# A two-layer expert kernel: the early conditional cast of first-layer weights goes into one arm of the first layer

## The chip, the cores and the metric

The kernel runs on one core of one Trainium2 chip. The metric is the device time of one execution in microseconds (us), the median of several runs.

## The reference

Three layers follow each other: a gated linear attention, a first feed-forward layer (a maximum of three products, then an output product), and a mixture of experts in which each token goes to the one expert whose gate is largest. The change lies in the last.

```python
B, H, S, D = 4, 8, 768, 48                      # attention
state = alpha_t[..., None] * state + k_t (outer) v_t ;  y_t = q_t @ state
x = y.transpose(0, 2, 1, 3).reshape(3072, 384)
x = np.maximum(np.maximum(x @ w1, x @ w2), x @ w3) @ w_out      # 384 -> 768 -> 384

logits = x @ w_gate                              # experts: 8, d_ff = 1024
e_idx = np.argmax(logits, axis=1)
gate_w = probs[np.arange(N), e_idx]              # softmax
eom = 1.0 / (1.0 + np.exp(-(x @ w_output_gate)))
for e in range(8):
    mask = e_idx == e
    h = np.maximum(x[mask] @ w1[e], 0.0)         # 384 -> 1024
    out[mask] = gate_w[mask, None] * eom[mask, e, None] * (h @ w2[e])
```

## The kernel before

The first 484 us compute attention and the first feed-forward layer. The rest is a loop over *slots* `j`: a slot is up to 128 tokens of one expert, in the order of the experts. There are at most `NS` = 31 slots; with these inputs 30 are used, and how many tokens each expert has is known only on the chip.

Products are made in one of two ways. In a slot of more than 64 tokens (*whole*), weights and activations are split into a high and a low part in the fast 32-bit format, and three products stand for one: high by high, high by low, low by high. The split weights of the first layer are `w1H` and `w1L`, one pair of buffers for all slots; `split1` makes them from the staging buffer `s1` by 6 pieces, each a copy on ScalarE (ACT, line 605) and a subtraction on VectorE (DVE, line 606). `w2H`, `w2L`, `s2` and `split2` (8 pieces) do the same for the second layer. A slot whose tokens fit in 64 (*alone*) needs no split weights: it multiplies straight from `s1` and `s2` in plain 32-bit, both halves of the width side by side (`halves`, line 814). Staging buffers are two of each kind, `s1a`/`s1b` and `s2a`/`s2b`, used in turn by even and odd slots, and filled by DMAs that SyncE (SP) issues only if the slot's expert is another than the slot's before (line 775).

What a slot is stands in registers: `kind[j]` is 1 for an alone slot, and `new[j]` tells when the weights of a whole slot with a new expert may be cast: 0 not at all, 1 *late* (the slot before is whole and still reads `w1H`), 2 *early* (the slot before is alone and reads none of it). `cast1(j, when)` is `split1(j)` under `tc.If(new[j] == when)`. A conditional has two arms in the program. In the arm that is skipped, ACT and DVE wait until all that they issued before is finished, and then raise the semaphore by as much as the other arm would have; whoever waits for a cast thus waits for that point where there is no cast.

The order on each engine is the order of the code (`manual_schedule`). One pass of the loop, for slot `j`:

1. `split2(j)`, pieces 0 and 1 (under a conditional, line 1152)
2. `up(j + 1, 0)`: first half of the next slot's first layer, 9 products of TensorE (PE, line 825) into a bank `psM`, copied by ACT (line 826) to `hs`. An alone slot has nothing here.
3. `th(j)`: transposes of `hs` (8 on PE, line 865; 4 in an alone slot, line 870), then ReLU and split into `ch` by two instructions each on ACT (line 844) and DVE (line 845); in an alone slot one ReLU on ACT (line 871)
4. `split2(j)`, pieces 2 to 7 (conditional, line 1162)
5. `cast1(j + 2, 2)`, the early cast (conditional; the records show line 1132 for it)
6. `up(j + 1, 1)`: second half, 9 products, or all 12 of an alone slot (line 814)
7. `tx(j + 2)`: 3 transposes of the gathered tokens (line 788), then `cx` high by ACT (line 793) and low by DVE (line 794)
8. DMA of `s1` of slot `j + 3`
9. `cast1(j + 2, 1)`, the late cast (conditional, line 1132 too)
10. `down(j)`: second layer, 24 products (line 884) or 16 (line 814), scaling by ACT (line 898), for an alone slot one addition of halves (lines 902, 903), and a scatter to the output by GpSimd (POOL, line 904)
11. DMA of `s2` of slot `j + 2`

All `up` products of a whole slot read `w1H` and `w1L`, so they wait for the last place in the program before them that may have written these.

Of the kernel before, what the change touches and what calls it, by code (L numbers as in the profile page):

```python
# [33 lines left out]
NS = NT + NE - 1  # L34
# [50 lines left out]
def layers(tc, pool, wk, K, general, *args):  # L85
    with ExitStack() as ctx:
        _layers(ctx, tc, pool, wk, K, general, *args)


def _layers(ctx, tc, pool_, wk, K, general, qk, al, a0, v, vT, w123, wout, gates, ew1, ew2, out):  # L90
# [25 lines left out]
    def bank(p, tag, name):  # L116
        return p.tile([128, 512], F32, tag=tag, name=name)
# [460 lines left out]
    xg, cx, cxF, hs, ch, chg, new, eos, kind = ({} for _ in range(9))  # L578
# [25 lines left out]
    def split(src, hi, lo):  # L604
        nc.scalar.copy(hi, src)
        nc.vector.tensor_sub(lo, src, hi.bitcast(F32))

    def split1(j, pieces=range(6)):
        for n in pieces:
            split(*(t[:, n % 3, n // 3 * 512:(n // 3 + 1) * 512] for t in (C["s1"][j % 2], *C["w1"])))  # L610

    def split2(j, pieces=range(NE)):
        for f in pieces:
            split(*(t[:, f] for t in (C["s2"][j % 2], *C["w2"])))
# [148 lines left out]
    def load_meta(j):  # L763
        chg[j] = nc.values_load(kinds[0:1, 2 * NS + j:2 * NS + j + 1], engines=(ET.SP,), min_val=0, max_val=1)
        eos[j] = nc.values_load(meta[0:1, j:j + 1], engines=(ET.SP,), min_val=0, max_val=NE - 1)

    def load_kind(j):
        kind[j] = nc.values_load(kinds[0:1, j:j + 1], engines=(ET.PE, ET.Activation, ET.DVE),
                                 min_val=0, max_val=1)
        new[j] = nc.values_load(kinds[0:1, NS + j:NS + j + 1], engines=(ET.Activation, ET.DVE),  # L770
                                min_val=0, max_val=2)
# [6 lines left out]
    def gather(j):  # L778
        xg[j] = C["cr"].tile([128, XW], F32, tag="xg", name="xg", bufs=4)
        n = TF * 128 if j < NF else NTOK  # L780
        nc.gpsimd.indirect_dma_start(out=xg[j], out_offset=None, in_=x2d[:n, :],
                                     in_offset=bass.IndirectOffsetOnAxis(ap=gidx[:, j:j + 1], axis=0),
                                     bounds_check=n - 1, oob_is_err=False)

    def tx(j):
        ps = bank(C["psT"], "T", "psT")
        for k in range(3):
            nc.tensor.transpose(ps[:, k * 128:(k + 1) * 128], xg[j][:, k * 128:(k + 1) * 128], ident)
        cx[j] = bp.tile([128, 2, DM], F32R, tag=("xH", "xL")[j % 2], name="cx")
        cxF[j] = bp.tile([128, DM], F32, tag="hH", name="cxF", bufs=7)  # L790

        def parts(hi, lo, p):
            nc.scalar.copy(hi, p)
            nc.vector.tensor_sub(lo, p, hi.bitcast(F32))  # L794

        def alone():
            nc.scalar.copy(cxF[j], ps[:, :DM])

        by_kind(j, lambda: parts(cx[j][:, 0], cx[j][:, 1], ps[:, :DM]), alone)

    def by_kind(j, whole, alone):
        if j not in kind:
            return whole()
        with tc.If(kind[j] == 1) as c:
            alone()
        with c.Else():
            whole()
# [4 lines left out]
    def halves(ps, n, x, w, start, stop):  # L812
        for g in range(2):
            mm(ps[64 * g:64 * g + 64, :n], x[g], w[g], start=start, stop=stop, skip_group_check=True)

    def up(j, h):
        w1H, w1L = C["w1"]
        fs = slice(h * 512, h * 512 + 512)

        def whole():  # L820
            ps = bank(psM, "M", "psM1")
            for k in range(3):
                ks = slice(k * 128, (k + 1) * 128)
                for n, (x, w) in enumerate(((0, w1H), (0, w1L), (1, w1H))):
                    mm(ps, cx[j][:, x, ks], w[:, k, fs], start=(k + n == 0), stop=(k + n == 4))  # L825
            nc.scalar.copy(hs[j][:, fs], ps)  # L826

        def alone():
            ps = bank(psM, "M", "psM1")
            w = C["s1"][j % 2]  # L830
            for k in range(3):
                x = cxF[j][:, k * 128:k * 128 + 64]
                halves(ps, 512, (x, x), [w[:, k, g * 512:(g + 1) * 512] for g in range(2)], k == 0, k == 2)
            nc.scalar.copy(hs[j][:, :512], ps)

        if h == 0:
            hs[j] = bp.tile([128, FF2], F32, tag="x32", name="hs")
            with tc.If(kind[j] == 0) if j in kind else nullcontext():
                whole()
        else:  # L840
            by_kind(j, whole, alone)
# [14 lines left out]
    def th(j):  # L856
        ch[j] = bp.tile([128, 2, FF2], F32R, tag=f"o{j % 2}", name="ch", bufs=1)
        p0 = bank(C["psH"], "H", "psH")

        def whole():  # L860
            p1 = bank(C["psH"], "H", "psH")
            for h, ps in enumerate((p0, p1)):
                for f in range(4):
                    fs = slice((4 * h + f) * 128, (4 * h + f + 1) * 128)
                    nc.tensor.transpose(ps[:, f * 128:(f + 1) * 128], hs[j][:, fs], ident)
                cut(ch[j][:, 0, h * 512:h * 512 + 512], ch[j][:, 1, h * 512:h * 512 + 512], ps)

        def alone():
            for f in range(4):
                nc.tensor.transpose(p0[:, f * 128:(f + 1) * 128], hs[j][:, f * 128:(f + 1) * 128], ident)  # L870
            nc.scalar.activation(hs[j][:, 512:], p0, AF.Relu)

        by_kind(j, whole, alone)

    def down(j, fs=(0, NE)):
        if fs[0] == 0:
            C["dn"] = bank(psM, "M", "psP") if j == 1 else bank(psO, "O", "psP")
        ps = C["dn"]
        w2H, w2L = C["w2"]

        def whole():
            for f in range(*fs):
                for n, (x, w) in enumerate(((0, w2H), (0, w2L), (1, w2H))):
                    mm(ps[:, :DM], ch[j][:, x, f * 128:(f + 1) * 128], w[:, f], start=(f + n == 0),  # L884
                       stop=(f == NE - 1 and n == 2))

        def alone():
            w = C["s2"][j % 2]
            for f in range(4):
                x = hs[j][:, 512 + f * 128:512 + (f + 1) * 128]  # L890
                halves(ps, DM, (x[:, :64], x[:, 64:]), (w[:, f], w[:, f + 4]), f == 0, f == 3)

        by_kind(j, whole, alone)
        if fs[1] < NE:
            return
        y = bp.tile([128, DM], F32, tag="hm", name="yo")
        gate = xg[j][:, DM:XW]
        nc.scalar.activation(y, ps[:, :DM], AF.Copy, scale=gate)  # L898
        if j in kind:
            with tc.If(kind[j] > 0):  # L900
                t = bp.tile([128, DM], F32, tag="hL", name="ylo", bufs=7)
                nc.scalar.copy(t[:64], ps[64:, :DM])
                nc.vector.scalar_tensor_tensor(y[:64], t[:64], gate[:64], y[:64], op0=ALU.mult, op1=ALU.add)
        nc.gpsimd.indirect_dma_start(out=out[:, :], out_offset=bass.IndirectOffsetOnAxis(ap=sidx[:, j:j + 1], axis=0),  # L904
                                     in_=y, in_offset=None, bounds_check=NTOK - 1, oob_is_err=False)
# [222 lines left out]
    def guard(j):  # L1128
        return tc.If(n_all > j) if j >= NT else nullcontext()

    def cast1(j, when):
        with tc.If(new[j] == when):  # L1132
            split1(j)

    down(1, (0, 2))
    tx(2)
    down(1, (2, 5))
# [9 lines left out]
    for j in range(NF, NS):  # L1147
        if j + 3 < NS:
            load_meta(j + 3)
            load_kind(j + 3)  # L1150
        if j > NF:
            with tc.If(new[j] > 0):
                split2(j, range(2))
        if j + 3 < NS:
            gather(j + 3)
        with guard(j):  # L1156
            if j + 1 < NS:
                with guard(j + 1):
                    up(j + 1, 0)
            th(j)  # L1160
        if j > NF:
            with tc.If(new[j] > 0):
                split2(j, range(2, NE))
        if j + 2 < NS:
            cast1(j + 2, 2)
        if j + 1 < NS:
            with guard(j + 1):
                up(j + 1, 1)
                if j + 2 < NS:
                    tx(j + 2)  # L1170
        if j + 3 < NS:
            stage(j + 3, ((0, "s1"),))
        if j + 2 < NS:
            cast1(j + 2, 1)
        with guard(j):  # L1175
            down(j)
        if j + 2 < NS:
            stage(j + 2, ((1, "s2"),))
# [50 lines left out]
```

## Time and profile before

| what | us |
|---|---|
| median of 3 runs (834.53, 840.00, 840.49) | 840.0 |
| the profiled execution | 835.41 |
| its span, from the first to the last instruction | 833.7 |
| PE busy in that span | 746.9 (90%) |
| ACT busy | 307.0 (37%) |
| DVE busy | 380.9 (46%) |

The mean granted clock of PE over the span is 0.957 of full speed; in the slices of the page's second part that fall in the loop it reads 8 or 9 tenths in many, where the stages before it read 9. A matmul's recorded time is longer than the step to the next one, because matmuls overlap; the pace is read from the starts. A row of the timeline names the start, the time, the engine, the line, the operation and its tiles, and in brackets how long the engine stood idle just before and what ended that.

### The profile page before, as it was taken

The page shows a single profiled execution, that of the slowest core. Times are in us where ns is not written, and L with a number is a line of the kernel's source. Part 1 is how long each engine was busy: PE and PEld are TensorE (multiplying, and loading weights), DVE is VectorE, ACT ScalarE, POOL GpSimd, SP SyncE. Part 2 cuts the span into 40 slices and gives each one's busy share as a digit, 9 for nine tenths or more (in the row PEclk, how much of TensorE's full clock was granted, in tenths as well). Part 3 has the DMA queues.
Part 4 walks back from the last instruction along what each step waited for, and adds up shares of the span by engine and source line. Part 5 has one row for each costly group of instructions (what it writes and reads, how often), then busy time and mean ns, then how long its engine had stood idle before and what let it go on. Part 6 is the DMA issues. An engine that isn't in the chain of part 4 may idle for free. (4 is left out here: it accounts for less than half of the span.)

```text
span 833.7 us, 14691 instructions
## 1 busy us (share of the span) xinstructions
PE 746.9 (90%) x4782; PEld 652.7 (78%) x4782; DVE 380.9 (46%) x806; ACT 307.0 (37%) x750; POOL 110.7 (13%) x117
## 2 busy tenths in 40 slices
PE   7889999989999999999999888888879798896882
PEld 7679989878999999999999777777556577763562
DVE  7868784598676474632327621110232311102322
ACT  4364343544434343432314422222444422324342
POOL 1000000010111110100103021011211201111110
PEclk9999999998999999999999999898989989999897
DMA  9732302624104140000004010115936101377450
GB/s 256 293 87 91 131 0 77 183 67 115 54 18 121 37 120 20 17 12 20 8 28 181 23 56 30 30 39 175 335 119 249 32 20 39 114 282 306 145 212 15
DMA packets 23748, 86.63 MB, mean 104 GB/s; under 512 B 7988, under 2 KB 11852, under 8 KB 19536
## 3 DMA queue, kind: packets, MB, share of 16 engines
q1 hardware_dynamic: 18192, 73.24, 26.5%
q0 software_dynamic: 3904, 10.84, 4.1%
q10 hardware_dynamic: 1536, 1.18, 0.6%
q8 instruction: 51, 0.84, 0.4%
q14 instruction: 65, 0.53, 0.2%
HBM read 128.09 MB, written 10.63 MB: 166 GB/s over the span
## 5 line engine op out<-in xcount | busy, mean ns | idle before, releaser
L429 PE MATMUL hps<-xH,wH 128*128 128x384 f32 x432 | 151.4, 350 | 1.8 <-ACT xH L341 1.8
L429 PE MATMUL hps<-xH,wL 128*128 128x384 f32 x432 | 146.1, 338 | 0.7 <-DVE wL L398 0.7
L429 PE MATMUL hps<-xL,wH 128*128 128x384 f32 x432 | 146.2, 339 | 0.4 <-DVE xL L342 0.4
L825 PE MATMUL psM<-w1H,cx 128*128 128x512 f32 x276 | 108.0, 448 | 36.6 <-ACTq L1132 36.6
L884 PE MATMUL psP<-w2H,ch 128*128 128x384 f32 x368 | 103.2, 351 | 1.4 <-ACT ch L844 1.3
L825 PEld LDWEIGHTS psM<-w1H,cx 128*128 128x128 f32 x276 | 57.6, 209 | 56.3 <-ACTq L1132 43.2
L455 POOL TENSOR_TENSOR hL<-hm,hH 128x384 fp32r<-128x384 f32 x36 | 44.8, 1244 | 404.6 <-ACT hH L450 404.5
L429 PEld LDWEIGHTS hps<-xH,wH 128*128 128x128 f32 x432 | 82.1, 190 | 8.4 <-ACT xH L341 2.5
L845 DVE SCALAR_TENSOR_TENSOR ch<-psH,ch 128x512 fp32r<-128x512 f32 x46 | 29.7, 686 | 128.6 <-ACT ch L844 128.2
L429 PEld LDWEIGHTS hps<-xH,wL 128*128 128x128 f32 x432 | 82.2, 190 | 1.0 <-DVE wL L398 1.0
L429 PEld LDWEIGHTS hps<-xL,wH 128*128 128x128 f32 x432 | 82.2, 190 | 0.9 <-DVE xL L342 0.9
L884 PEld LDWEIGHTS psP<-w2H,ch 128*128 128x128 f32 x368 | 69.8, 195 | 2.0 <-ACT ch L844 1.5
L826 ACT COPY hs<-psM 128x512 f32<-128x512 f32 x46 | 26.9, 586 | 117.2 <-PE psM L825 115.3
L825 PE MATMUL psM<-w1L,cx 128*128 128x512 f32 x138 | 62.4, 452 | 7.9 <-DVEq L1132 7.8
L465 PE MATMUL ops<-wo,hH 128*128 128x400 f32 x258 | 68.2, 345 | 0.0
L904 POOL DMA_INDIRECT out<-yo,sidx x30 | 31.2, 1041 | 275.0 <-ACTq L900 161.5
L884 PE MATMUL psP<-w2L,ch 128*128 128x384 f32 x184 | 63.1, 343 | 0.0
L436 DVE TENSOR_TENSOR hm<-hm,hps 128x384 f32<-128x384 f32 x48 | 26.4, 551 | 67.0 <-PE hps L429 63.0
L794 DVE TENSOR_TENSOR cx<-psT,cx 128x384 fp32r<-128x384 f32 x24 | 13.3, 556 | 89.0 <-ACTq L1132 88.9
L450 ACT CAST hH<-hm 128x384 fp32r<-128x384 f32 x43 | 22.0, 512 | 80.9 <-DVE hm L439 77.2
L898 ACT ACTIVATE yo<-psP,xg 128x384 f32<-128x384 f32 x30 | 17.4, 581 | 88.5 <-PE psP L884 65.2
L465 PEld LDWEIGHTS ops<-wo,hH 128*128 128x128 f32 x258 | 46.9, 188 | 0.4
(214 smaller groups left out, 1200.9 us busy)
## 6 DMA issues: line engine op xcount, KB each, us to landing
s1a<-in_ew SPq DMA_DIRECT2D x15, 1536.0 KB
s2a<-in_ew SPq DMA_DIRECT2D x15, 1536.0 KB
s1b<-in_ew SPq DMA_DIRECT2D x14, 1536.0 KB
s2b<-in_ew SPq DMA_DIRECT2D x14, 1536.0 KB
ws<-in_w SPq DMA_DIRECT2D x6, 1152.0 KB
at<-in_al SPq DMA_DIRECT2D x16, 336.9 KB
vt<-in_v SPq DMA_DIRECT2D x8, 576.0 KB
x2d<-xs SPq DMA_DIRECT2D x24, 192.0 KB
```

The costliest lines, as they stand in the source:

```text
L429: mm(ps, slab(a, f)[:, w, k], b[i][:, k], start=(n == 0), stop=(n == 8))
L436: nc.vector.tensor_max(m, m, ps)
L450: nc.scalar.copy(hH[i, f], m)
L455: (nc.gpsimd if general or i > 1 else nc.vector).tensor_sub(hL[i, f], hps["m"], hH[i, f].bitcast(F32))
L465: mm(ps[:, :DM + NG], a[i, f][:, ts_], wo[f // 3][:, b, f % 3], start=(f + n == 0), stop=(f + n == 7))
L794: nc.vector.tensor_sub(lo, p, hi.bitcast(F32))
L825: mm(ps, cx[j][:, x, ks], w[:, k, fs], start=(k + n == 0), stop=(k + n == 4))
L826: nc.scalar.copy(hs[j][:, fs], ps)
L845: nc.vector.scalar_tensor_tensor(lo, ps, 0.0, hi.bitcast(F32), op0=ALU.max, op1=ALU.subtract)
L884: mm(ps[:, :DM], ch[j][:, x, f * 128:(f + 1) * 128], w[:, f], start=(f + n == 0), stop=(f == NE - 1 and n == 2))
L898: nc.scalar.activation(y, ps[:, :DM], AF.Copy, scale=gate)
L904: nc.gpsimd.indirect_dma_start(out=out[:, :], out_offset=bass.IndirectOffsetOnAxis(ap=sidx[:, j:j + 1], axis=0), in_=y, in_offset=None, bo ...
```

## The change

`cast1` is defined further up, and its early form is called in one other place: in the arm of `up(j, 1)` that an alone slot takes, behind its products and their copy. There it is `cast1(j + 1, 2)`, for the slot after it. The call between `split2` and `up(j + 1, 1)` in the loop goes. The late form stays where it was. Since `new[j] == 2` holds only where slot `j - 1` is alone, the same casts are made as before.

```diff
+    def cast1(j, when):
+        with tc.If(new[j] == when):
+            split1(j)
+
     def up(j, h):
...
             nc.scalar.copy(hs[j][:, :512], ps)
+            if j + 1 < NS:
+                cast1(j + 1, 2)
...
-    def cast1(j, when):
-        with tc.If(new[j] == when):
-            split1(j)
-
...
                 split2(j, range(2, NE))
-        if j + 2 < NS:
-            cast1(j + 2, 2)
         if j + 1 < NS:
             with guard(j + 1):
                 up(j + 1, 1)
```

On ACT, between the two ReLU instructions of `th` and the copy that ends `up(j + 1, 1)`, the order before is this (L1162 is the conditional of `split2`, L1132 that of the early cast, L804 the choice between alone and whole; a branch that waits for ACT's own semaphore is the end of a skipped arm):

```order
L844 ACTIVATE ch<-psH 128x512 [waits PE_49]
L804 UNCONDITIONAL_BRANCH
L1162 COMPARE_AND_BRANCH
L605 CAST w2H<-s2a 128x384 [waits DMAHW3_49,DVE_49,Activation_49]
L605 CAST w2H<-s2a 128x384 [waits DVE_49,Activation_49] x5
L1162 UNCONDITIONAL_BRANCH
L1162 UNCONDITIONAL_BRANCH [waits Activation_49]
L1132 COMPARE_AND_BRANCH
L605 CAST w1H<-s1a 128x512 [waits DMAHW4_49,DVE_49,Activation_49]
L605 CAST w1H<-s1a 128x512 [waits DVE_49,Activation_49] x5
L1132 UNCONDITIONAL_BRANCH
L1132 UNCONDITIONAL_BRANCH [waits Activation_49]
```

The products of the whole arm that follow read `w1H`, and this last skipped arm is the point that they wait for. In the changed kernel the same stretch of ACT, on to the copies, is this (lines are shifted: L850 is L844 before, L1164 is L1162, L817 is L1132, L838 the copy of an alone slot, L830 that of a whole one):

```order
L850 ACTIVATE ch<-psH 128x512 [waits PE_49]
L804 UNCONDITIONAL_BRANCH
L1164 COMPARE_AND_BRANCH
L605 CAST w2H<-s2a 128x384 [waits DMAHW3_49,DVE_49,Activation_49]
L605 CAST w2H<-s2a 128x384 [waits DVE_49,Activation_49] x5
L1164 UNCONDITIONAL_BRANCH
L1164 UNCONDITIONAL_BRANCH [waits Activation_49]
L804 COMPARE_AND_BRANCH
L838 COPY hs<-psM_5819 128x512 [waits PE_49,Activation_49]
L817 COMPARE_AND_BRANCH
L605 CAST w1H<-s1a 128x512 [waits DMAHW4_49,DVE_49]
L605 CAST w1H<-s1a 128x512 [waits DVE_49] x5
```

The cast now stands behind the alone arm's copy, inside the choice of L804. A whole slot's products stand in the other arm of that choice; the last write of `w1H` ahead of them is the one of the pass before (its late cast, or the early cast of its alone arm). On DVE the choice of L804 around `up(j + 1, 1)` had no work before; now it holds the six subtractions:

```order
L1164 UNCONDITIONAL_BRANCH [waits DVE_49]
L804 COMPARE_AND_BRANCH
L817 COMPARE_AND_BRANCH
L606 TENSOR_TENSOR w1L<-s1a,w1H 128x512 [waits DMAHW4_49,PE_49,Activation_49]
L606 TENSOR_TENSOR w1L<-s1a,w1H 128x512 [waits PE_49,Activation_49] x2
L606 TENSOR_TENSOR w1L<-s1a,w1H 128x512 [waits Activation_49] x3
L817 UNCONDITIONAL_BRANCH
L817 UNCONDITIONAL_BRANCH [waits DVE_49]
L804 UNCONDITIONAL_BRANCH [waits DVE_49]
```

The last branch is new: in a whole slot DVE waits for its own work there and raises its semaphore by six, behind nothing that PE's products of that arm wait for.

## Rows read from the trace of the kernel before

**Rows 1.** The page, busy time of each engine, share of the span, instructions.

```profile
PE 746.9 (90%) x4782; PEld 652.7 (78%) x4782; DVE 380.9 (46%) x806; ACT 307.0 (37%) x750; POOL 110.7 (13%) x117
```

**Rows 2.** Who waited for whom, PE: us in total, times, longest us.

```profile
PE psM L825 <- ACTq L1132: 36.6, 23, 3.6
PE psM L825 <- DVEq L1132: 7.8, 18, 0.7
```

**Rows 3.** Timeline of one pass, slot 8: start, us, engine, line; brackets: idle before.

```profile
569.01 0.40 PE L825 MATMUL psM<-w1H,cx 128*128 128x512 f32 x1
...
571.11 1.03 PE L865 MATMUL psH<-ident,hs 128*128 128x128 f32 x8
...
571.85 1.09 ACT L844 ACTIVATE ch<-psH 128x512 fp32r<-128x512 f32 x2
572.48 1.29 DVE L845 SCALAR_TENSOR_TENSOR ch<-psH,ch 128x512 fp32r<-128x512 f32 x2 [6.36 <-ACT ch L844]
...
573.28 0.49 PE L825 MATMUL psM<-w1H,cx 128*128 128x512 f32 x1 [1.14 <-ACTq L1132]
...
574.19 0.50 PE L825 MATMUL psM<-w1L,cx 128*128 128x512 f32 x1 [0.42 <-DVEq L1132]
...
577.21 0.85 PE L788 MATMUL psT<-ident,xg 128*128 128x128 f32 x3
```

**Rows 4.** Timeline of PE, two stretches without idle time.

```profile
476.32 1.11 PE L853 MATMUL psH<-ident,hs 128*128 128x128 f32 x8
477.19 0.43 PE L884 MATMUL psP<-w2H,ch 128*128 128x384 f32 x1
...
499.35 0.49 PE L788 MATMUL psT<-ident,xg 128*128 128x128 f32 x3
499.59 0.42 PE L884 MATMUL psP<-w2H,ch 128*128 128x384 f32 x1
...
503.84 0.40 PE L825 MATMUL psM<-w1H,cx 128*128 128x512 f32 x1
```

**Rows 5.** Windows over 16 passes: length; PE, PEld, DVE, ACT, POOL busy; PEclk; DMA; GB/s.

```profile
494.62:503.84 9.22, 7.98 (x45) 7.03 (x44) 1.84 (x3) 2.54 (x5) 0.80 (x1) 1.00 0.15 44
...
557.85:569.01 11.16, 9.61 (x45) 8.21 (x44) 1.84 (x3) 2.54 (x5) 1.02 (x1) 0.85 0.42 142
...
778.45:793.49 15.04, 11.03 (x45) 9.08 (x43) 5.13 (x10) 5.56 (x13) 2.38 (x2) 0.77 0.37 128
sum 180.50, PE 147.52 PEld 126.71 DVE 38.82 ACT 49.77 POOL 19.96; mean PE 9.22 PEld 7.92 DVE 2.43 ACT 3.11 POOL 1.25
```

**Rows 6.** Timeline of PE at a skipped arm, an alone slot's products, and behind an alone `th`.

```profile
582.95 1.07 PE L865 MATMUL psH<-ident,hs 128*128 128x128 f32 x8 [0.56 <-PEq L838]
583.95 2.80 PE L814 MATMUL psM<-s1a,cxF 128*64 128x512 f32 x12
...
605.99 0.50 PE L825 MATMUL psM<-w1H,cx 128*128 128x512 f32 x1 [1.05 <-ACTq L1132]
```

**Rows 7.** Timeline of DVE at the split of second-layer weights, slot 26.

```profile
781.29 2.89 DVE L606 TENSOR_TENSOR w2L<-s2a,w2H 128x384 fp32r<-128x384 f32 x6
```

**Rows 8.** Timeline around the early cast for slot 15: ACT, then DVE, then PE.

```profile
631.04 3.23 ACT L605 CAST w1H<-s1b 128x512 fp32r<-128x512 f32 x6 [0.26 <-DVE ch L845]
634.18 0.57 ACT L834 COPY hs<-psM 128x512 f32<-128x512 f32 x1
...
631.96 3.70 DVE L606 TENSOR_TENSOR w1L<-s1b,w1H 128x512 fp32r<-128x512 f32 x6 [0.34 <-PE psM L814]
635.58 0.55 DVE L794 TENSOR_TENSOR cx<-psT,cx 128x384 fp32r<-128x384 f32 x1
...
628.92 2.79 PE L814 MATMUL psM<-s1a,cxF 128*64 128x512 f32 x12
...
636.26 0.39 PE L825 MATMUL psM<-w1H,cx 128*128 128x512 f32 x1
```

**Rows 9.** Timeline of ACT at the early cast for slot 26.

```profile
760.80 3.22 ACT L605 CAST w1H<-s1a 128x512 fp32r<-128x512 f32 x6 [4.76 <-DMA s1a<-in_ew]
```

## The prediction, made before the changed kernel ran

> **What bounds the kernel now.** I read the page first: PE is busy 746.9 us of the 833.7 us span, far ahead of DVE and ACT [rows 1]. So PE sets the time, and only two things can make it shorter: PE's idle time, and stretches in which PE works at half speed and is counted as busy all the same.
>
> The view of waits says where PE idles. Two lines lead it by far, and both are first-layer products (line 825) that wait at line 1132, the conditional cast: 36.6 us in 23 waits for ACT and 7.8 us in 18 waits for DVE [rows 2]. There are only four early casts in the whole run, so most of these are waits for a conditional that does nothing.
>
> The timeline of one pass shows how [rows 3]. The eight transposes start at 571.11. ACT makes its two ReLUs until 572.94. The second half of the next slot's first layer could have started right behind the transposes, but its first product starts at 573.28, after 1.14 us idle, put down to ACT's conditional; the first product with `w1L` then loses another 0.42 us to DVE's. The reason is the skipped arm: ACT may raise the semaphore for the cast that it does not make only when its ReLUs are done, and DVE only after its two subtractions. The products need nothing of either; their weights have been there since an earlier slot.
>
> Second, the speed. The nine products before the transposes go from 569.01 to 571.11, 2.10 us. The nine behind the wait go from 573.28 to 577.21, 3.93 us with 0.42 us idle in it: some 3.5 us for the same work [rows 3]. [...]
>
> **The change, part by part.**
>
> *The wait that goes.* In the changed order a whole slot's second half no longer has a cast, skipped or not, between it and the transposes. The last one ahead of it is that of the pass before, which lies behind a whole set of second-layer products, over 4 us earlier. What would such a pass take? From rows without idle time: eight transposes 477.19 - 476.32 = 0.87; nine products 2.10 [rows 3]; three transposes 499.59 - 499.35 = 0.24; 24 second-layer products 503.84 - 499.59 = 4.25 [rows 4]. Sum 7.46 us from the first transpose to the end of the second layer.
>
> The run has 16 passes of this kind (a whole slot's transposes, a whole slot's second half behind them). I took a window for each, from its first transpose to the next slot's first product, or, in four where an alone slot follows, to the last product's end (0.16 us later). They sum to 180.50 us [rows 5]. Without the wait and at full speed they would take 16 x 7.46 + 4 x 0.16 = 120.0 us. Gain 60.5 us. Of this 180.50 - 147.52 = 33.0 us is PE idle in these windows, and the other 27.5 us is the lower clock.
>
> *What is late next.* Behind the second half come the transposes of tokens and then the second layer, which waits for `ch` and for the skipped arm of `split2`. In the pass of slot 8 the second layer would start 0.87 + 2.10 + 0.24 = 3.2 us after the first transpose, at 574.3; DVE's last subtraction ends at 573.77 [rows 3], and only the products from the third group on, 1.1 us later still, need DVE's skipped arm. That leaves half a microsecond or more, so nothing takes the wait's place. In the three passes in which `split2` really casts, the wait was 3 us and more (longest 3.6 [rows 2]), because the early cast's skipped arm stood behind six casts. Take slot 26: its first transpose is at 778.45 [rows 5], the second layer could start at 781.7 and needs its eight pieces one after another, about 0.53 us apart, the third at 782.8 and the last at 785.4. DVE makes pieces three to eight from 781.29 to 784.18 [rows 7]: each in time. So these waits go whole.
>
> *Four passes behind an alone slot's transposes.* There the second half idles 1.05 us for the same skipped arm [rows 6]; there are four, 1.05 to 1.08 us each. Gain 4.2 us.
>
> *Waits that stay.* Three of the 23 waits are those of a first half (`up(j + 1, 0)`), for a late cast's arm or for a cast really made. They stay.
>
> *The four casts that are moved.* They now come behind the alone slot's copy. For slots 12 and 26 ACT stands waiting for the staging DMA before the cast (the longer, 4.76 us, is shown [rows 9]); the copy, 0.57 us, fits into that wait, and the cast still starts when the DMA lands: 0. The SP queue's order is unchanged, and its DMAs for these two come at the same distance from the products that free the buffers. For slots 15 and 29 the weights are there early. For slot 15 the cast starts at 631.04 before the alone products (628.92 + 2.79 = 631.71) are out; now copy (0.57) and cast come behind them, so the cast starts near 632.5, 1.45 us later. DVE's six subtractions (3.70) and its `cx` follow it and end near 637.6 instead of 636.13; the first half of slot 15 stands ready at 636.26 [rows 8] and its second product needs them. Cost 1.1 us; the same at slot 29. Bounds: 0 if the copy is overlapped by the cast, 1.45 each plus one stretch at the lower clock (27.5 / 16 = 1.7) at most. I take 2.2 for both.
>
> *Branches.* ACT and DVE pass one conditional less in whole slots; DVE gets a new skipped arm at the end of `up(j + 1, 1)`, with only its own `cx` subtraction behind it, which nobody needs for 4 us. PE's jump into the whole arm used to lie under the wait, so its cost is not seen. Nearest rows: an alone slot's products follow the transposes with no idle time across the same branches, and where PE skips an arm and must first let its own work end, it idles 0.56 us [rows 6]. The whole arm has no such end. I take 0, with 20 x 0.56 = 11 us as the upper bound; a gain is excluded, since a jump is not shorter than none.
>
> [...]
>
> Sum: 60.5 + 4.2 - 2.2 = 62.5 us. The profiled execution took 835.4, so 772.9; from the median of 840.0 it is 777.5. The three runs lie at 834.5 and 840.0 to 840.5, so I take a point nearer the median: 776.
>
> **The rivals.**
>
> *The clock does not come back.* The waits go but the same stretches stay at the lower level. For it: not every wait is followed by it (passes at 1.00 have the same wait of about 1.1 us), so the trace does not tie it to the wait alone. Against: in the pass shown the products ahead of the wait run at full pace, 2.10 us for nine, and the slow ones begin right behind it [rows 3]; I found no pass of the loop in which they begin anywhere else. Time: 776 + 27.5 = 803.
>
> *The jump costs what a skipped arm costs.* 20 second halves at 0.56 us: 776 + 11 = 787. For it: nothing shows this jump bare. [...]
>
> *The change does not do what it says.* The products of the whole arm still stop for ACT or DVE, at a wait that lay hidden under this one (a bank, a copy). For it: PE waits on semaphores that only count, and a count can be reached later than the work it stands for. Against: three banks in turn, whose copies lie a half slot back. Time as before, between the profiled execution's 835 and the median of 840: 838.
>
> *Slower: the casts end up on the path.* The waits stay as in the last rival, and at slots 15 and 29 copy, casts and `cx` follow each other bare, 0.57 + 3.23 + 0.55 = 4.35 us, each with 1.7 us of clock: 840 + 12 = 852; it decides as soon as the gain of the whole slots is under these 12 us. For it: DVE and ACT work in the same conditional that PE passes. Against: the 33 us of idle time would have to find a new cause.
>
> **How the numbers follow.** Forecast 0.70, jump 0.08, clock 0.13, nothing done 0.05, slower 0.04. A measurement of this kernel tells about 1% from no change. Faster by over 1%: 0.70 + 0.08 + 0.13 = 0.91; within 1%: 0.05; slower 0.04. The range goes from 766 (both bounds of the moved casts at their good end, and the low run of 834.5) to 804, which takes in the clock rival.
>
> **What would show it.** Right: the waits of PE at line 825 for the conditional cast fall from 44 us to about 8, at first halves only; the passes of whole slots shrink to 7.5 us from their first transpose, with a granted clock of 1.00; the mean clock of the loop rises; at slots 15 and 29 about 1 us of waiting is new. Wrong: a new waiter in the same place, whatever it names; passes near 9.2 us with no idle time in them (the clock rival); or an idle 0.5 us ahead of each second half put down to PE's own sequencer (the jump).

## The result and the profile after

The changed kernel takes 772.2 us (median of 4 runs, 770.0 to 773.3), the kernel before in the same comparison 837.9 (4 runs, 834.5 to 840.5). The ratio is 0.9215, 95% interval 0.917 to 0.926. Forecast were 776.0 us and a range of 766 to 804. The profiled execution took 773.25 us with a span of 771.3, so span against span (833.7) the gain is 62.4 us.

The page of the changed kernel, busy time of each engine and the granted clock in 40 slices:

```profile
PE 720.7 (93%) x4782; PEld 639.6 (83%) x4782; DVE 380.7 (49%) x806; ACT 306.6 (40%) x750; POOL 111.0 (14%) x117
...
PEclk9999999998999999999999999999999999999996
```

The work is the same, 4782 instructions on PE, DVE and ACT as busy as before [rows 1], but PE is busy 26.2 us less. Most of that is put down to the clock, by an estimate from the mean granted clocks: they fall short of full speed by (1 - 0.957) x 833.7 = 35.8 us before and by (1 - 0.979) x 771.3 = 16.2 us after, so at most some 20 us of the 26.2 come from it. The rest is a price of stopping that is not counted as idle time, about 0.5 us a pass; the windows below show it. The other 36.2 of the 62.4 us are idle time of PE that is gone.

What the lower clock was in the kernel before, a window in the slow half of slot 8's pass shows (length; PE, PEld, DVE, ACT, POOL busy; granted clock; DMA; GB/s):

```profile
576.00:578.00 2.00, 2.00 (x8) 1.62 (x7) 0.00 (x0) 0.49 (x1) 0.00 (x0) 0.50 0.00 0
```

PE is busy in all of it, at a granted clock of 0.50. The first-layer products start 0.42 to 0.43 us apart there (575.08 to 577.21); ahead of the pass's transposes it was 0.23 to 0.24 us (569.01 to 571.11).

Who waited for whom, PE at its first-layer products (now line 829; the conditional cast is now line 817):

```profile
PE psM L829 <- ACTq L817: 4.9, 3, 2.2
PE psM L829 <- DVEq L817: 2.7, 4, 0.7
```

Of 36.6 us in 23 waits and 7.8 us in 18 [rows 2], 7.6 us in 7 waits are left, all of them at first halves. The pass that [rows 3] shows, slot 8, in the timeline of PE, then of ACT, then of DVE (products are line 829, transposes 871, ReLU and split into `ch` 850 and 851, the second layer 890):

```profile
549.59 0.40 PE L829 MATMUL psM<-w1H,cx 128*128 128x512 f32 x1
...
551.68 1.03 PE L871 MATMUL psH<-ident,hs 128*128 128x128 f32 x8
552.47 0.48 PE L829 MATMUL psM<-w1H,cx 128*128 128x512 f32 x1
...
554.65 0.49 PE L788 MATMUL psT<-ident,xg 128*128 128x128 f32 x3
554.90 0.42 PE L890 MATMUL psP<-w2H,ch 128*128 128x384 f32 x1
...
552.42 1.09 ACT L850 ACTIVATE ch<-psH 128x512 fp32r<-128x512 f32 x2
...
553.06 1.29 DVE L851 SCALAR_TENSOR_TENSOR ch<-psH,ch 128x512 fp32r<-128x512 f32 x2 [6.19 <-ACT ch L850]
```

The second half starts at 552.47, 0.79 us behind the first transpose, where it took 2.17 us before; no row of PE has a wait. DVE is done with `ch` at 554.35, half a microsecond before the second layer starts at 554.90.

The windows over the 16 passes, as in [rows 5] (length; PE, PEld, DVE, ACT, POOL busy; granted clock; DMA; GB/s); first and last, and the sum:

```profile
494.15:501.61 7.46, 7.46 (x45) 7.01 (x44) 1.85 (x3) 2.55 (x5) 0.80 (x1) 1.00 0.17 55
...
722.36:729.99 7.63, 7.63 (x45) 6.86 (x43) 5.12 (x10) 5.38 (x13) 2.39 (x2) 1.00 0.56 203
sum 120.46, PE 120.46 PEld 112.00 DVE 38.80 ACT 48.81 POOL 19.98; mean PE 7.53 PEld 7.00 DVE 2.42 ACT 3.05 POOL 1.25
```

180.50 us became 120.46, PE has no idle time in any of the 16, and the clock is 1.00 in all.

The first pass shows what a stop costs beside its idle time. Its clock was 1.00 before as well [rows 5], and still PE's busy time fell from 7.98 to 7.46 us. So a pass with 9.22 - 7.98 = 1.24 us of idle time lost 9.22 - 7.46 = 1.76. Part of the difference can be read off: eight transposes count as 1.03 us of busy time where PE stops behind them, but the next product starts 0.79 us after the first of them where PE does not stop (551.68 to 552.47). Five of the 16 passes had the clock at 1.00 before, and in each the busy time fell by about 0.5 us.

What is left or new, in the timeline of PE at slots 12, 15, 26 and 29 and at the last slot's second layer:

```profile
576.88 0.49 PE L829 MATMUL psM<-w1H,cx 128*128 128x512 f32 x1 [1.38 <-ACTq L817]
578.12 0.79 PE L829 MATMUL psM<-w1L,cx 128*128 128x512 f32 x1 [0.75 <-DVEq L817]
...
606.98 0.50 PE L829 MATMUL psM<-w1L,cx 128*128 128x512 f32 x1 [0.62 <-DVEq L817]
...
709.73 0.50 PE L829 MATMUL psM<-w1H,cx 128*128 128x512 f32 x1 [2.15 <-ACTq L817]
710.97 0.70 PE L829 MATMUL psM<-w1L,cx 128*128 128x512 f32 x1 [0.75 <-DVEq L817]
...
740.10 0.50 PE L829 MATMUL psM<-w1L,cx 128*128 128x512 f32 x1 [0.59 <-DVEq L817]
...
751.13 0.44 PE L890 MATMUL psP<-w2H,ch 128*128 128x384 f32 x1 [1.66 <-ACT ch L850]
```

The waits at slots 15 and 29 are new, 0.62 and 0.59 us of idle time. The same places of the kernel before, slots 12 and 26 and the last slot:

```profile
600.39 0.49 PE L825 MATMUL psM<-w1H,cx 128*128 128x512 f32 x1 [1.85 <-ACTq L1132]
601.16 0.50 PE L825 MATMUL psM<-w1L,cx 128*128 128x512 f32 x1 [0.27 <-DVEq L1132]
...
764.97 0.49 PE L825 MATMUL psM<-w1H,cx 128*128 128x512 f32 x1 [3.44 <-ACTq L1132]
765.73 0.55 PE L825 MATMUL psM<-w1L,cx 128*128 128x512 f32 x1 [0.27 <-DVEq L1132]
...
814.96 0.44 PE L884 MATMUL psP<-w2H,ch 128*128 128x384 f32 x1 [1.29 <-ACT ch L844]
```

### The profile page after: what moved, and what is told of

Read it like the earlier page. It is cut to its first block, busy times and chain, and to the rows that moved or that the text cites. A ratio compares the mean times of both kernels' runs of the same rounds, so it can differ in the third digit from the quotient of the medians.

```text
span 771.3 us, 14622 instructions
## 1 busy us (share of the span) xinstructions
PE 720.7 (93%) x4782; PEld 639.6 (83%) x4782; DVE 380.7 (49%) x806; ACT 306.6 (40%) x750; POOL 111.0 (14%) x117
## 5 line engine op out<-in xcount | busy, mean ns | idle before, releaser
L829 PE MATMUL psM<-w1H,cx 128*128 128x512 f32 x276 | 98.5, 412 | 4.9 <-ACTq L817 4.9
L890 PE MATMUL psP<-w2H,ch 128*128 128x384 f32 x368 | 101.3, 346 | 1.8 <-ACT ch L850 1.7
L890 PEld LDWEIGHTS psP<-w2H,ch 128*128 128x128 f32 x368 | 67.9, 190 | 2.3 <-ACT ch L850 1.9
L829 PEld LDWEIGHTS psM<-w1H,cx 128*128 128x128 f32 x276 | 53.3, 193 | 18.9 <-ACTq L817 6.5
L890 PE MATMUL psP<-w2L,ch 128*128 128x384 f32 x184 | 62.4, 339 | 0.0
L829 PE MATMUL psM<-w1L,cx 128*128 128x512 f32 x138 | 56.3, 408 | 2.8 <-DVEq L817 2.7
L830 ACT COPY hs<-psM 128x512 f32<-128x512 f32 x46 | 27.1, 588 | 64.5 <-PE psM L829 62.8
L465 PE MATMUL ops<-wo,hL 128*128 128x400 f32 x129 | 44.3, 343 | 0.1
```

What stands on the lines that cost most here:

```text
L465: mm(ps[:, :DM + NG], a[i, f][:, ts_], wo[f // 3][:, b, f % 3], start=(f + n == 0), stop=(f + n == 7))
```

## The experiments

Two theories. **A**: the time went into a conditional that did nothing, between the transposes and the whole second half, and into the lower clock behind it. **B**: it went into the place of the four casts that are really made. The rival of A's second half is that the lower clock has a cause of its own. Except for e3's added products, which nobody reads, no kernel here does more or less work than the changed one. Each is compared with runs of the kernel before on the same chip: 836.7 us for e1 to e4 (17 runs), 835.5 for e5 and e6 (13), 835.3 for e7 to e9 (11).

**e1: no early cast at all.** The casts that were early are made late, where the others are.

```diff
-    def cast1(j, when):
-        with tc.If(new[j] == when):
+    def cast1(j):
+        with tc.If(new[j] > 0):
...
-            if j + 1 < NS:
-                cast1(j + 1, 2)
...
-            cast1(j + 2, 1)
+            cast1(j + 2)
```

> The changed kernel without any early cast: its call in the alone arm is taken out, and the late cast takes every new expert (new[j] > 0). Theory A (the gain is the skipped conditional that no longer stands between the transposes and a whole slot's second half): the passes of whole slots stay as in the changed kernel, 9.6 us apart. For the four slots that had an early cast, the cast now follows the cast of the tokens, and the first half of the slot needs only the first pieces when it starts: the waits of 1.4 + 0.75 us (slot 12), 2.2 + 0.75 us (slot 26) and 0.6 us each (slots 15 and 29) should go, and some 1.6 us at the lower clock behind each of the first two, together about 9 us: 763 against 772. Theory B (the gain comes from the place of the four casts, early being better than late): they come later still, so 772 or more, up to 772 + 4 x 4 = 788.

Measured: 763.9 us (762.8 to 769.6, 6 runs), ratio 0.9155 (0.9114 to 0.9197). The waits of PE, then the timeline of PE at slot 26:

```profile
PE psM L829 <- ACTq L817: 1.4, 1, 1.4
```

```profile
703.94 0.50 PE L829 MATMUL psM<-w1H,cx 128*128 128x512 f32 x1
704.66 0.50 PE L829 MATMUL psM<-w1L,cx 128*128 128x512 f32 x1 [0.23 <-DVE w1L L606]
```

The one wait for the conditional that is left is the loop's first. At slot 26 PE now waits for the cast pieces themselves, 0.23 us instead of 2.15 + 0.75. With every cast later the kernel is faster than both, so B falls: no early place of the casts is needed, and their early place costs (e8 repeats the comparison on one chip).

**e2: the do-nothing conditional put back.** The changed kernel, with a cast that is never made where the early one stood (`new` is never 3).

```diff
             with tc.If(new[j] > 0):
                 split2(j, range(2, NE))
+        if j + 2 < NS:
+            cast1(j + 2, 3)
         if j + 1 < NS:
```

> The changed kernel with a conditional cast put back at the old place, under new[j] == 3, which never holds: no cast is ever made there, and the four real ones stay in the alone arm. Theory A: PE waits 1.1 us again before each whole second half, 3.3 us and more where split2 works, and runs the lower clock behind many of them: back to 838, plus the 1.2 us that the moved casts cost, 836 to 842. Theory B: as the changed kernel, 772.

Measured: 835.2 us (830.3 to 838.3, 10 runs), ratio 0.998 (0.995 to 1.001): the whole gain is gone. The waits of PE:

```profile
PE psM L829 <- ACTq L817: 34.4, 23, 3.6
PE psM L829 <- DVEq L817: 9.5, 20, 0.7
```

They are nearly those of [rows 2] again, though the four casts stand at their new place. A is shown: an arm that no run enters costs 63 us (835.2 against 772.2).

**e3: PE kept busy through the wait.** The kernel before, with 12 products of the identity by itself ahead of each whole second half.

```diff
         def whole():
+            if h == 1 and j in kind:
+                fill = bank(C["psR"], "R", "fill")
+                for _ in range(12):
+                    mm(fill[:, :128], ident, ident, start=True, stop=True)
             ps = bank(psM, "M", "psM1")
```

> The kernel before, with 12 products of the identity into a bank that nobody reads, ahead of the 9 products of a whole slot's second half, in PE's idle time: about 12 x 0.15 = 1.8 us for 1.14 + 0.42 us of waiting. The waits for the conditional stay, only PE is not idle in them. If the lower clock follows PE's idle time: the 11 passes at the lower clock go back to full speed except where the wait is over 3 us, some 8 to 9 passes x 1.7 us = 14 us less, and some 0.2 us more for each of 20 passes: 838 - 14 + 4 = 828, and windows of whole passes near 9.8 us at clock 1.00. If the clock has another cause: the same stretches stay at the lower level, 838 to 842.

Measured: 826.3 us (825.2 to 830.0, 4 runs), ratio 0.989 (0.984 to 0.995). The timeline of PE in one pass, and the window of that pass from one slot's transposes to the next's:

```profile
505.99 1.04 PE L869 MATMUL psH<-ident,hs 128*128 128x128 f32 x8
506.87 2.84 PE L824 MATMUL fill<-ident 128*128 128x128 f32 x24
509.47 0.47 PE L829 MATMUL psM<-w1H,cx 128*128 128x512 f32 x1
```

```profile
505.99:518.27 12.28, 12.28 (x78) 11.39 (x77) 1.85 (x3) 3.12 (x6) 2.05 (x3) 1.00 0.12 35
```

The useless products (each counted as two instructions) take 2.60 us (506.87 to 509.47), 0.22 us each where 0.15 was expected, longer than the 1.14 + 0.42 us of idle time that they fill, and the kernel is 1.1% faster all the same. The clock is 1.00 in 15 of the 16 passes; the lower level is left in slot 26's pass, where PE still waits 0.91 + 0.73 us behind the filler, and at the last slot. So with PE's idle time filled the lower clock is gone from 10 of the 11 passes that had it before. The expectation was 828 us for this side and 838 to 842 for the other.

**e4 and e6: the do-nothing conditional on one engine alone.** e4 puts the never-entered arm back with work for ACT only, e6 with work for DVE only.

```diff
+        if j + 2 < NS:
+            with tc.If(new[j + 2] == 3):
+                for n in range(6):
+                    nc.scalar.copy(*(t[:, n % 3, n // 3 * 512:(n // 3 + 1) * 512] for t in (C["w1"][0], C["s1"][j % 2])))
```

In e6 the loop is this one:

```diff
+                for n in range(6):
+                    w = slice(n // 3 * 512, (n // 3 + 1) * 512)
+                    nc.vector.tensor_sub(C["w1"][1][:, n % 3, w], C["s1"][j % 2][:, n % 3, w], C["w1"][0][:, n % 3, w].bitcast(F32))
```

> The changed kernel with a conditional at the old place that never holds and has work for ACT alone (six copies into w1H), none for DVE. Theory A: PE waits for ACT's skipped arm, 1.1 us before each whole second half (33 us of idle time in 16 passes becomes some 1.1 x 13 + 3.3 x 3 + 1.1 x 4 = 29 us), and the lower clock follows in part: 800 to 835. If DVE's later arm was what cost, and ACT's comes in time: near 772 + 5.

> The changed kernel with a conditional at the old place that never holds and has work for DVE alone (six subtractions into w1L), none for ACT. DVE's skipped arm comes about 0.6 us after ACT's, so PE makes one product and then stands idle about 1.8 us at the first product with w1L, once, where the conditional with both engines gives 1.14 + 0.42. If the clock falls with the length of the idle time: more of the 16 passes at the lower clock than with ACT alone (3 of 16), as many as before (11) or more; time 830 to 842. If the clock falls because the idle time comes in two pieces, few of the passes are at the lower clock: 815 to 822.

Measured: e4 812.3 us (809.7 to 814.2, 4 runs), ratio 0.971 (0.966 to 0.977); e6 831.6 us (829.3 to 835.6, 10 runs), ratio 0.997 (0.995 to 0.999). The waits of PE in e4, then in e6:

```profile
PE psM L829 <- ACTq L1167: 29.6, 20, 3.6
```

```profile
PE psM L829 <- DVEq L1167: 37.9, 17, 4.9
```

The windows from one slot's transposes to the next's; a pass like the first ones takes 9.60 us in the changed kernel (503.71 to 513.31). Two of e2, then three of e4 (the third has a real `split2`), then two of e6:

```profile
505.99:519.23 13.24, 11.69 (x54) 9.91 (x53) 1.85 (x3) 3.19 (x6) 2.03 (x3) 0.87 0.11 32
532.45:544.14 11.69, 10.14 (x54) 8.75 (x53) 1.85 (x3) 3.12 (x6) 2.05 (x2) 1.00 0.12 36
```

```profile
506.16:517.16 11.00, 9.87 (x54) 8.73 (x53) 1.85 (x3) 3.12 (x6) 2.04 (x3) 1.00 0.13 39
517.16:528.13 10.97, 9.83 (x54) 8.69 (x53) 1.85 (x3) 3.13 (x6) 2.07 (x3) 1.00 0.12 37
602.01:615.36 13.35, 9.44 (x46) 7.99 (x44) 5.12 (x10) 5.72 (x13) 2.21 (x2) 0.87 0.39 133
```

```profile
505.60:517.30 11.70, 9.89 (x55) 8.71 (x54) 1.85 (x3) 3.12 (x6) 2.04 (x3) 1.00 0.12 36
528.94:542.40 13.46, 11.35 (x54) 9.81 (x53) 1.84 (x3) 3.13 (x6) 2.04 (x2) 0.87 0.10 32
```

PE's busy time on the pages of e2 and of e4:

```profile
PE 747.8 (90%) x4782; PEld 651.9 (78%) x4782; DVE 380.9 (46%) x806; ACT 307.5 (37%) x750; POOL 111.0 (13%) x117
```

```profile
PE 730.8 (90%) x4782; PEld 643.5 (79%) x4782; DVE 381.0 (47%) x806; ACT 306.6 (38%) x750; POOL 110.7 (14%) x117
```

Either engine alone makes PE wait, each for its own skipped arm. ACT's arm costs about 1.14 us of idle time in a pass (1.4 us of its length, 11.00 for 9.60) and leaves the clock of the 16 passes at 1.00, except in the three with a real `split2`, as the third window of e4 shows. DVE's costs about 1.8 us, behind one product, and the clock falls in 12 of the 16 passes. e6 was to tell whether the clock falls because the idle time comes in two pieces (815 to 822 us) or with its length (830 to 842, 11 passes or more): 831.6 us and 12 passes stand on the side of the length. From e2 to e4 the span falls by 24.4 us (834.4 to 810.0), of which PE's busy time is 17.0: mostly clock (some 15, by the same estimate from the granted clocks, 0.957 and 0.974), for 0.42 us of waiting in a pass. From e4 to the changed kernel it falls by 38.7 (to 771.3), of which busy time is 10.1: mostly idle time.

**e5: the early cast ahead of the copy.** In the changed kernel's alone arm the two change places.

```diff
-            nc.scalar.copy(hs[j][:, :512], ps)
             if j + 1 < NS:
                 cast1(j + 1, 2)
+            nc.scalar.copy(hs[j][:, :512], ps)
```

> The changed kernel with the early cast ahead of the copy of hs in the alone arm, not behind it. If the wait of 0.6 us each at slots 15 and 29 is the price of standing behind the alone products and their copy (the prediction's term, put at 1.1 us each), it should go or fall under 0.2 us at both, and at slots 12 and 26, where the cast waits for its DMA, the copy and the tokens' cast come 0.5 us later, so the first product there waits some 0.5 us longer: in sum 772 give or take 1, which only the two waits in the profile tell from the changed kernel. If the 0.6 us has another cause (the DMA, or the subtractions of DVE), it stays.

Measured: 768.6 us (767.0 to 769.5, 4 runs), ratio 0.920 (0.918 to 0.922). In the timeline the waits at slots 15 and 29 are gone, as expected (0 and 0.03 us). At slot 26 there is one wait of 3.43 us instead of 2.15 and 0.75; at slot 12 the first wait stayed at 1.38 us, where 0.5 more was expected, and the second fell from 0.75 to 0.26. But the total fell 3.6 us, more than was expected, and the chips were not the same. So e7 to e9 compare three kernels on one chip.

**e7, e8, e9: the changed kernel, e1 and e5 again, side by side.**

> The changed kernel once more, beside the next two on the same chip, since its first times came from another. About 772 us, ratio to before 0.92. Idle time of PE as in the first profile: slot 12 about 1.4 + 0.75 us, slot 15 0.6, slot 26 about 2.2 + 0.75, slot 29 0.6, in sum about 6.3 us; lower clock behind the waits of slots 12 and 26.

> The kernel without early casts (e1_late_only) once more, for a comparison with the changed kernel on one chip. If the early casts cost what PE's waits at slots 12, 15, 26 and 29 show (some 6 us of idle time and one or two stretches at the lower clock of 1.7 us each), it is 6 to 10 us faster than e7_after_again. Rival: the difference of the first runs was one of the chips, then the two agree within 3 us.

> The early cast ahead of the copy (e5_cast_first) once more. By the waits alone it gains 1.2 us at slots 15 and 29 and loses about 0.8 at slot 26, so it agrees with e7_after_again within 2 us. Rival: it is 3 to 4 us faster again, and then a stretch at the lower clock behind slot 12 that e7_after_again has and this one has not, or another place, must show it.

| kernel | median, us (6 runs each) | ratio to before, 95% interval |
|---|---|---|
| e7, the changed kernel | 771.4 (771.2 to 772.9) | 0.925 (0.922 to 0.928) |
| e8, no early cast (e1) | 765.6 (761.9 to 768.9) | 0.9185 (0.915 to 0.922) |
| e9, cast ahead of the copy (e5) | 768.0 (765.3 to 771.3) | 0.920 (0.916 to 0.923) |

The kernel without early casts is 5.9 us faster than the changed one, just under the 6 to 10 that were expected, and no run of the one reaches a run of the other. e9 is 3.4 us faster again, so its expected 2 us was too little. A part of the rest that both pairs show lies at the end: the windows over the last slot's second layer, 24 products, in the kernel before, the changed kernel, e5 and e9:

```profile
814.96:820.01 5.05, 4.93 (x24) 4.06 (x24) 4.08 (x8) 2.90 (x7) 0.74 (x1) 1.00 0.02 4
```

```profile
751.13:757.53 6.40, 6.29 (x24) 5.64 (x24) 4.07 (x8) 2.89 (x7) 0.44 (x1) 0.73 0.03 7
```

```profile
747.42:752.48 5.06, 4.95 (x24) 4.07 (x24) 4.08 (x8) 2.90 (x7) 0.74 (x1) 1.00 0.02 5
```

```profile
750.62:755.65 5.03, 4.92 (x24) 4.06 (x24) 4.08 (x8) 2.90 (x7) 0.74 (x1) 1.00 0.02 5
```

In the changed kernel (e7 too) the last slot waits 1.66 us and then runs at a granted clock of 0.73 (e7: 0.74); before it waited 1.29, in e5 and e9 1.36, and ran at 1.00. That is 1.6 us of the gain. The waits at slots 15 and 29 are 1.4 us, counted from start to start; at slot 26 e5 and e9 wait 0.5 and 0.8 us longer in sum. So some 2 to 2.5 us of the 3.4 have a place. The place that e9's rival named, the clock at slot 12, does not belong to either kernel. The windows from the alone slot's second layer to the end of slot 12's first half, in e7, then in e9:

```profile
572.96:580.18 7.22, 5.25 (x26) 2.81 (x26) 4.78 (x8) 4.96 (x10) 0.00 (x0) 1.00 0.83 302
```

```profile
573.81:582.89 9.08, 6.64 (x27) 3.86 (x26) 4.78 (x8) 5.14 (x10) 0.90 (x1) 0.81 0.83 313
```

Here it is e9 that has the lower clock and a longer wait, 1.9 us in all, while between the first profiles of the same two kernels it was the changed kernel that had it (clock 0.81) and e5 that had not (1.00). So e9's profiled execution, the longest of its six (771.25 us), is no shorter than e7's (771.51), and the 3.4 us stand on the medians. ACT stands idle for 0.65 us ahead of the last slot's `ch` in the changed kernel and in e7, put down to DVE's pieces of `w2L`; before, in e5 and in e9 it is 0.35 us, put down to ACT's own skipped arm. Why was not tried.

## Why the prediction was right, point by point

- **What bounds it**: right. PE set the time, and the two waits of [rows 2] with what followed them were the gain; e2 brings all of it back with one conditional that is never entered.
- **The 16 passes**: 120.0 us was worked out from rows at full pace [rows 4], 120.46 came. The 33.0 us of idle time are gone as well. The other 27.5 us were mis-sized as clock: by the granted clock of the 16 windows before (11.16 x 0.15 = 1.7 us in the second row of [rows 5], and so on) some 20 us are clock at most, and the rest is the price of stopping that the first pass shows above, about 0.5 us a pass. The sum was not touched by it, since both went with the waits. The 1.7 us for one stretch at the lower clock (27.5 / 16) agrees with 11.16 x 0.15 by luck, as only 11 of the 16 passes had such a stretch.
- **What is late next**: nothing, as worked out. In the three passes with a real `split2` the last one takes 7.63 us (722.36 to 729.99) and PE waits nowhere in it.
- **The four passes behind an alone slot's transposes**: the 1.05 to 1.08 us [rows 6] are gone; no such wait stands in the view after. The 4.2 us were too little: from the first transpose to the second half it was 1.68 us or more before and is 0.39 or less now, 1.3 to 1.8 us in each.
- **Waits that stay**: the three at first halves stayed, 4.9 us where they were 6.7 (1.37, 1.85 and 3.44).
- **Casts at slots 12 and 26, 0**: the first product's wait fell (1.85 to 1.38 us, 3.44 to 2.15), since the copy, 0.48 us from its start to the next (763.92 to 764.40 at slot 26 before), no longer stands between the cast and ACT's share of `cx`; the second product's rose (0.27 to 0.75 each). The sum is as before at slot 12 (2.13 for 2.12) and smaller at slot 26 (2.90 for 3.71): zero was right. The smaller wait at slot 26 is no gain, since PE now waits longer before that, ahead of the transposes of the gathered tokens (1.05 us, put down to nothing that the profile shows, for 0.44, put down to the tokens' DMA): from the alone products to the end of that first half it took 14.6 us before (754.50 to 769.07) and 14.5 after (699.94 to 714.46).
- **Casts at slots 15 and 29, 1.1 us each**: somewhat too much. PE's idle time is 0.62 and 0.59 us; from start to start slot 15's nine products take 2.98 us (605.97 to 608.95) where they took 2.09 (636.26 to 638.35), and slot 29's 2.96 where they took 2.19: 0.9 and 0.8 us. The timeline of the changed kernel at slot 15, PE's alone products, slot 15's first product and the transposes behind its nine, then ACT, then DVE:

```profile
598.63 2.80 PE L814 MATMUL psM<-s1a,cxF 128*64 128x512 f32 x12
...
605.97 0.40 PE L829 MATMUL psM<-w1H,cx 128*128 128x512 f32 x1
...
608.95 0.60 PE L876 MATMUL psH<-ident,hs 128*128 128x128 f32 x4
...
601.56 0.59 ACT L838 COPY hs<-psM 128x512 f32<-128x512 f32 x1 [0.72 <-PE psM L814]
602.05 3.22 ACT L605 CAST w1H<-s1b 128x512 fp32r<-128x512 f32 x6
...
602.70 3.70 DVE L606 TENSOR_TENSOR w1L<-s1b,w1H 128x512 fp32r<-128x512 f32 x6 [1.03 <-ACT w1H L605]
606.32 0.55 DVE L794 TENSOR_TENSOR cx<-psT,cx 128x384 fp32r<-128x384 f32 x1
```

  The copy and the cast came as worked out: the copy begins 2.93 us after the first alone product (598.63), the cast 3.42 us after it; before it was 2.12 (631.04 against 628.92 [rows 8]), so the cast came 1.30 us later for the 1.45 predicted. The step that was too long is the next one, that DVE follows the cast by as much. DVE's subtractions start 4.07 us after the first alone product, before 3.04, so they came only 1.03 us later: before, they had themselves stood for 0.34 us behind PE's alone products [rows 8]. e5 confirms the term, since with the cast ahead of the copy both waits are gone.
- **A term that was missing**: the last slot. It lost 0.37 us of waiting (1.66 for 1.29) and 1.35 us of clock (6.40 us at 0.73 for 5.05 at 1.00), in e7 as well, and no step of the prediction had them.
- **Branches, 0**: right. PE's jump into the whole arm shows no idle time (552.47 follows the transposes at 551.68 by 0.79 us, no wait), as the jumps into the whole arms of the transposes and of the second layer had shown none before (571.11 [rows 3], 499.59 [rows 4]). So the second rival falls.
- **The clock rival**, 803: falls. In the changed kernel the clock is 1.00 in all 16 passes, and in e3 it is 1.00 in 15 of them with the conditional still there and only PE's idle time filled. Its price of 27.5 us was too high, as said above.
- **The sum**: 62.5 us predicted, 62.4 found between the two profiled executions, 65.7 between the medians of the comparison (837.9 and 772.2) and 63.8 between those of e7's (835.3 and 771.4). An agreement to 0.1 us is luck: the errors of the parts (four passes too small, the last slot missing, slots 15 and 29 too large) cancel within 2 us. The forecast of 776 lies 3.8 us above the median; 2 to 3 us of that are its starting point of 838.5, which lies so far above the medians of the 11 to 17 runs of the kernel before that the experiments brought (835.3 to 836.7).
- **The range**: its lower end does not come out of the terms given for it, 834.5 - 60.5 - 4.2 = 769.8 and not 766. The measured 772.2 lies above both.

## What to carry to other kernels

In these kernels a conditional that is not entered still has an end: each engine named in it says so in its own order, behind its own earlier work, and whoever waits for that end waits for that work (about 1.14 us a pass for ACT's in e4, 1.8 us for DVE's in e6, and 63 us in all for both in e2). Look for it in the view of waits as an engine's sequencer at the line of the conditional, and put such a conditional where the engines it names have nothing pending, or into an arm that is rarely taken. Price the idle time and the slower work behind it separately: here the idle time was little more than half of the loss (36.2 of 62.4 us). And the idle time in brackets was not the whole price of a stop even at a granted clock of 1.00: the first pass lost 1.76 us for 1.24 us of it.

## What the runs showed of the hardware that was not expected

The lower clock became more frequent with the idle time in a pass, but idle times of one length gave either level. Counted over the 13 passes without a real `split2`, from the granted clock behind the wait:

| kernel | PE's idle time in a pass | passes with the lower clock |
|---|---|---|
| changed kernel | none | 0 of 13 |
| e4 | 1.14 us (0.89 to 1.38) ahead of the nine products | 0 of 13 |
| before, e2 | 1.14 us ahead, about 0.4 us more behind the first | 8 of 13 each |
| e6 | 1.8 us (1.5 to 2.1) behind the first | 9 of 13 |

In the three passes with a wait of 3.3 us and more ahead of the products it fell every time, in before, e2 and e4 alike. In the others equal waits gave either level, and in e3 the first half of slot 26 waited 2.65 + 0.26 us and its products ran at 1.00. Two of the passes side by side: the first of e2's windows above has 1.13 + 0.42 us and a clock of 0.87, the second 1.14 + 0.41 and 1.00. What decides between two such passes stays open. What had not been expected at all is e4: the longer wait, for ACT, left the clock up where it stood alone, and adding the shorter one, for DVE, brought most of the clock's loss (mean granted clock 0.979 in the changed kernel, 0.974 in e4, 0.957 in e2).
